# Masking one block of attention rows by multiplication instead of by bias matmuls, in a fused attention and feed-forward kernel

## The chip, the cores and the metric

The kernel runs on one core of a Trainium2 chip. The time is that of one execution on the device, in microseconds (us). TensorE, VectorE, ScalarE, GpSimd and SyncE appear in the profile as PE, DVE, ACT, POOL and SP; PEld is TensorE's weight load.

## The reference

Attention with a band mask of 96 keys, 8 global keys and a slope per head, then a feed-forward layer with a squared ReLU. Cut to what matters:

```python
batch, n_heads, seq, head_dim = (4, 8, 768, 64);  n_global, n_local = (8, 96)
scores = scale * q @ k.T                      # scale = 1/8
dist   = where(is_global & ~is_local, n_local, abs(rel))
scores = where(is_global | is_local, scores - slopes[h] * dist, -1e9)
x = (softmax(scores) @ v)                     # -> (3072, 512)
h = x @ w_in                                  # 512 x 2048
g = s * maximum(h, 0)**2 + b
out = g @ w_out                               # 2048 x 512
```

## The kernel before

The work is cut into 12 **granules** of 256 query rows, three for each of the four batches. They are numbered 0 to 11. The first of each batch (0, 3, 6, 9) has 3 blocks of 128 score columns for each head, the others 4. A **head pair** is two heads; four pairs make a granule. Bias and mask come in one of two ways. Granules 0 and 1 add them in PSUM with a bias matmul ahead of the scores (`SB_mm`); later granules multiply the exponentiated scores by a table `tmpl = exp(slope * base)` on VectorE (`S_mul`), because that table takes time to build and VectorE is free later.

```python
def SB_mm(j, hp, which=None):            # bias by TensorE: 768 or 1024 columns
    ...
    m = base[:].rearrange("p a c -> p (a c)")[:, c0 : c0 + n]
    for hi in range(2):
        nc.tensor.matmul(ps[:, hi, 0:n], lhsT=diag[:, 2 * hp + hi, :], rhs=m, start=True, stop=False)
def S_mul(j, hp):                        # mask by VectorE
    ...
    m = tmpl[:, 2 * hp : 2 * hp + 2, c0 : c0 + n]
    nc.vector.tensor_tensor(pt[:, :, 0:n], pt[:, :, 0:n], m, ALU.mult)
def P1(j, fp, sq="dve", tag="psh"):      # x @ w_in, slice fp of 8, for granule j
    for i in range(2):
        fc = 2 * fp + i
        for kc in range(KC):             # 8 matmuls of 256 columns in all
            nc.tensor.matmul(ps[:, i, :], lhsT=w_in_bf[:, kc, fc * P : (fc + 1) * P], rhs=xT[j][:, kc, :], ...)
    gs = gT[j][:, 2 * fp : 2 * fp + 2, :]
    nc.scalar.activation(gs, ps[:], ACT.Relu)
    ...                                  # and the square, on the engine that sq names
```

The schedule is written by hand: each engine runs its instructions in the order in which the program emits them. The loads of `w_in` come in eight slices, one for each `P1`:

```python
load_v(0); load_quads(1, "k"); load_quads(1, "q")
load_w_in(0, 8); load_w_in(1, 8); load_v(1)
for i in range(2, 8): load_w_in(i, 8)
load_quads(2, "k"); load_quads(2, "q"); load_v(2)
...
idle(9, "av")                            # nine matmuls on constants while the first loads come
...
SB_mm(1, 0);  P1(0, 0, "dve", "pso")     # granule 1's scores among granule 0's products with w_in
SB_mm(1, 1);  S_mm(1, 0, True); S_post(1, 0, True); S_mm(1, 1, True); S_post(1, 1, True)
P1(0, 1)
SB_mm(1, 2);  ...  SB_mm(1, 3);  ...
A(1, 0); A(1, 1, "pso"); P1(0, 2)        # A is P.V: probabilities times v
make_tmpl(0); make_tmpl(1)               # exp of 640 columns for one head, on ScalarE
A(1, 2); P1(0, 3); A(1, 3, "pso"); XT_half(1, 0, "act", "av"); P1(0, 4)
XT_half(1, 1, "dve", "pso"); P1(0, 5)
P1(1, 0); P1(1, 1); P1(1, 2); P1(1, 3)
make_tmpl(2); P1(0, 6)
T_quads(2, "k", ("pso", "av"))           # transposes of granule 2
```

The softmax here doesn't subtract the row's maximum and nothing guards it: scores larger than these inputs give would overflow.

## Time and profile before

| | before |
|---|---|
| time, median of 3 runs | 208.13 us (207.91 to 208.19) |
| span of the traced execution | 205.9 us |
| TensorE, VectorE, ScalarE busy | 97%, 82%, 57% |

The prediction below shows the lines that it rests on. A timeline row gives start, length, engine, line of the program, operation, operands and count; brackets hold the idle time ahead of it and what ended it.

```profile
5.85 0.82 PE L379 MATMUL ps_s<-base,diag 128*128 128x384 bf16 x4
9.29 0.54 PE L446 MATMUL ps_av<-vaug,pt 128*128 128x65 bf16 x12
...
28.13 0.55 PE L288 MATMUL ps_t<-ident,qnat 64*64 64x64 bf16 x32
```

```profile
27.27 0.69 DVE L306 COPY kT<-ps_t 128x512 bf16<-128x512 bf16 x1 [0.20 <-PE ps_t L288]
```

The four bias matmuls of the start take 0.82 us, the first P.V comes at 9.29, and VectorE takes up the transposed keys within 0.5 us of their start at 26.78. The second transposes, at 28.13, wait for nothing.

### The profile page before, as it was taken

Reading aid. Unit: us, or ns where it says so; the run is one execution under the profiler, and the core shown is the slowest. Engines: PE = TensorE matmul, PEld = TensorE weight load, DVE = VectorE, ACT = ScalarE, POOL = GpSimd, SP = SyncE. Lnnn points to the kernel's source line nnn. Section 1 sums busy time; section 2 is a strip of 40 time slices with the busy share of each in tenths; the row PEclk is TensorE's granted clock in tenths of the full one; section 3 lists DMA queues with packets and bytes.
Section 4 is the critical chain, followed back from the end, with each engine's and each line's share of the span. In section 5 each row is a group of like instructions: output and inputs, shape, how many; then the busy total and the mean of one; then the engine's idle time right before and its main releaser. Section 6 shows DMA issues by size and latency. Waiting matters only on the chain.

```text
span 205.9 us, 5605 instructions
## 1 busy us (share of the span) xinstructions
PE 199.9 (97%) x2291; PEld 161.0 (78%) x2299; DVE 169.1 (82%) x409; ACT 118.3 (57%) x181; POOL 73.7 (36%) x98
## 2 busy tenths in 40 slices
PE   7999999999999999999999999999999999999993
PEld 2667886547766678988988988988978988988883
DVE  3685576799989989788799799788799799787693
ACT  5779799455978586536446546546356446424400
POOL 8994673848273019009019029037000000000000
PEclk9999999999999999999999999999999999999999
DMA  5999999999999979999999969979946040050022
GB/s 165 194 183 198 190 194 193 182 148 162 134 125 155 211 112 102 188 159 129 190 128 106 208 82 117 204 114 119 194 80 178 3 135 21 0 153 3 2 105 102
DMA packets 103962, 27.64 MB, mean 134 GB/s; under 512 B 91392, under 2 KB 102016, under 8 KB 103936
## 3 DMA queue, kind: packets, MB, share of 16 engines
q0 software_dynamic: 70976, 13.11, 85.0%
q1 hardware_dynamic: 31904, 13.64, 34.2%
q10 hardware_dynamic: 1056, 0.52, 0.9%
q8 instruction: 18, 0.29, 0.6%
q14 instruction: 8, 0.07, 0.2%
HBM read 27.26 MB, written 6.29 MB: 163 GB/s over the span
## 4 chain that ended last, share of the span: by engine, by line
PE 83%; DVE 8%; ACT 3%; DMA 3%; issue 1%; POOL 0%; SPq 0%; DVEq 0%; ACTq 0%; POOLq 0%
PE ps L528 37%; PE ps_w L702 14%; PE ps_wb L702 6%; PE ps L589 6%; PE ps_av L446 5%; PE ps_s L395 5%; PE ps_wa L702 4%; ACT pt L408 2%; DMA raw<-in_k_dram 2%; PE ps_s L379 2%; DVE xn L464 2%; PE ps_2s L589 2%; DVE pt L418 2%; DMA xT<-xn 1%; DVE o_pr L627 1%
## 5 line engine op out<-in xcount | busy, mean ns | idle before, releaser
L528 PE MATMUL ps<-xT,w_in_bf 128*128 128x256 bf16 x768 | 96.6, 273 | 0.5 <-DVE xn L464 0.2
L528 PEld LDWEIGHTS <-w_in_bf 128*128 128x128 bf16 x768 | 72.7, 98 | 11.4 <-DVE xn L464 0.5
L540 ACT ACTIVATE gT<-ps 128x512 bf16<-128x512 f32 x72 | 43.1, 598 | 58.7 <-PE ps L528 55.9
L408 ACT ACTIVATE pt<-ps_s 128x1024 bf16<-128x1024 f32 (+1 forms) x48 | 43.1, 952 | 2.4 <-PE ps_s L395 2.4
L702 PEld LDWEIGHTS <-sw 128*128 128x128 bf16 x288 | 28.1, 98 | 3.4
L418 DVE TENSOR_TENSOR pt<-pt,tmpl 128x1024 bf16<-128x1024 bf16 (+1 forms) x40 | 25.1, 646 | 2.8 <-ACT pt L408 2.3
L556 DVE TENSOR_TENSOR gT<-gT 128x512 bf16<-128x512 bf16 x68 | 25.8, 415 | 1.8 <-ACT gT L540 1.6
L112 POOL DMA_DIRECT2D vaug<-in_v_dram x24 | 21.5, 913 | 3.9 <-DMA w_out_bf<-in_moe_w_out_dram 1.7
L702 PEld LDWEIGHTS <-gT 128*128 128x128 bf16 x208 | 19.7, 98 | 3.2 <-issue 0.2
L464 DVE TENSOR_TENSOR xn<-ps_av,rc 128x256 bf16<-128x256 f32 x48 | 20.4, 424 | 1.7
L125 POOL COPY pdum<-xT 1x1 bf16<-1x1 bf16 x5 | 3.0, 595 | 49.3 <-DMA xT<-xn 49.3
L589 PE MATMUL ps<-w_out_bf,gT 128*128 128x512 bf16 x74 | 18.8, 379 | 0.4 <-issue 0.2
L702 PE MATMUL ps_w<-tw,sw 128*128 128x256 bf16 x144 | 18.7, 273 | 0.0
L712 DVE SCALAR_TENSOR_TENSOR u<-ps_w,s_bc,bvec 128x256 f32<-128x256 f32 x27 | 12.9, 478 | 6.3 <-PE ps_w L702 6.3
L446 PEld LDWEIGHTS <-pt 128*128 128x128 bf16 x352 | 15.3, 98 | 3.6 <-DVE pt L418 1.2
L538 ACT ACTIVATE gT<-ps 128x512 bf16<-128x512 f32 x24 | 14.2, 599 | 5.1 <-PE ps L528 5.0
L104 POOL DMA_DIRECT2D qnat<-in_q_dram x18 | 16.0, 906 | 2.7 <-PE ps L528 1.8
L104 POOL DMA_DIRECT2D knat<-in_k_dram x18 | 15.9, 893 | 2.1 <-issue 1.6
L446 PE MATMUL ps_av<-vaug,pt 128*128 128x65 bf16 x224 | 16.4, 194 | 0.3 <-DVE pt L418 0.2
L463 DVE RECIPROCAL rc<-ps_av 128x4 f32<-128x4 f32 x48 | 8.7, 181 | 8.8 <-PE ps_av L446 8.5
L589 PEld LDWEIGHTS <-gT 128*128 128x128 bf16 x96 | 8.8, 98 | 8.1
L395 PE MATMUL ps_s<-qT,kT 64*128 64x128 bf16 x224 | 12.5, 218 | 0.0
(99 smaller groups left out, 240.8 us busy)
## 6 DMA issues: line engine op xcount, KB each, us to landing
out_dram<-o_pr SPq DMA_DIRECT2D x10, 512.0 KB, 5.9
vaug<-in_v_dram POOLq DMA_DIRECT2D x24, 128.0 KB, 7.9
knat<-in_k_dram POOLq DMA_DIRECT2D x22, 128.0 KB, 6.1
qnat<-in_q_dram POOLq DMA_DIRECT2D x22, 128.0 KB, 8.0
w_in_bf<-in_moe_w_in_dram POOLq DMA_DIRECT2D x8, 256.0 KB, 7.9
w_out_bf<-in_moe_w_out_dram POOLq DMA_DIRECT2D x4, 512.0 KB, 10.1
out_dram<-o_pr SPq DMA_DIRECT2D x3, 256.0 KB, 2.6
raw<-in_q_dram ACTq DMA_DIRECT2D x2, 256.0 KB, 4.8
```

The source lines that it names most:

```text
L104: nc.gpsimd.dma_start(t[:, i, :, :], src[b, :, sb * P : (sb + 1) * P, :].rearrange("h p d -> p h d"))
L112: nc.gpsimd.dma_start(vaug[b % 2][:, sb, :, 0:D], v[b, :, sb * P : (sb + 1) * P, :].rearrange("h p d -> p h d"),)
L395: nc.tensor.matmul(ps[:, hi, oc * P : (oc + 1) * P], lhsT=kt[r, :], rhs=qT[j][r, hp, i * P : (i + 1) * P], start=not biased, stop=not bias ...
L408: nc.scalar.activation(pt[:, :, 0:n], ps[:, :, 0:n], ACT.Exp, scale=QSCALE)
L418: nc.vector.tensor_tensor(pt[:, :, 0:n], pt[:, :, 0:n], m, ALU.mult)
L446: nc.tensor.matmul(av[:, i, hi, :], lhsT=pt[:, hi, c * P : (c + 1) * P], rhs=vv, start=n_ == 0, stop=n_ == len(ops) - 1,)
L464: nc.vector.tensor_tensor(xn[j][:, :, 2 * hp : 2 * hp + 2, :], av[:, :, :, 0:D], rc[:].to_broadcast((P, GB, 2, D)), ALU.mult,)
L528: nc.tensor.matmul(ps[:, i, :], lhsT=w_in_bf[:, kc, fc * P : (fc + 1) * P], rhs=xT[j][:, kc, :], start=(kc == 0), stop=(kc == KC - 1),)
L540: nc.scalar.activation(gs.rearrange("p f (r t) -> p f r t", r=2), ps[:].rearrange("p f (t r) -> p f r t", r=2), ACT.Relu,)
L556: nc.vector.tensor_tensor(gs, gs, gs, ALU.mult)
L589: nc.tensor.matmul(po[j, tb], lhsT=gT[j][:, fc, tb * P : (tb + 1) * P], rhs=w_out_bf[:, fc, :], start=(fc == 0), stop=(fc == FC - 1),)
L702: nc.tensor.matmul(wt[j, ps], lhsT=lhs[:, f, :], rhs=rhs[:, f, :], start=first and f == 0, stop=f == HF - 1, skip_group_check=True,)
```

## The change

The intent is to take eight bias matmuls off TensorE, the busiest engine, and to mask granule 1 on VectorE. The table must then exist sooner, so it is built by scaling the base for each head on VectorE and two large exps on ScalarE before 6 us; the last part follows in one exp later. Copies that granule 1's scores wait for are made in halves. The order of granule 0's products with `w_in` moves too. The four diagonals that ScalarE made go to VectorE as well, squares of granule 0 are put off (`"late"`, done later by `Q`), and some tiles change their place in PSUM.

```diff
-    base = const.tile([P, 5, P], BF16, name="base")
+    base = const.tile([P, 3, P], BF16, name="base")
...
+    def scale_base(lo, hi):
+        for h in range(H):
+            slope = float(2.0 ** (-8.0 * (h + 1) / H))
+            nc.vector.tensor_scalar_mul(tmpl[:, h, lo:hi, :], base[:, lo:hi, :], slope)
+    def make_tmpl(h0, h1, lo, hi):
+        t = tmpl[:, h0:h1, lo:hi, :]
+        nc.scalar.activation(t, t, ACT.Exp)
+    scale_base(1, 3)
+    make_tmpl(0, 4, 1, 3)
...
     def S_mul(j, hp):
+            m = m[:, :, 1:3, :].rearrange("p h a c -> p h (a c)")
+            x = pt[:].rearrange("p h (i c) -> p h i c", i=GB)
+            nc.vector.tensor_tensor(x, x, m.unsqueeze(2).to_broadcast((P, 2, GB, 2 * P)), ALU.mult)
...
-    SB_mm(1, 0)
-    P1(0, 0, "dve", "pso")
-    SB_mm(1, 1)
-    S_mm(1, 0, True)
-    S_post(1, 0, True)
...
+    S_mm(1, 0)
+    S_post(1, 0, mul=False)
+    P1(0, 0, "late", "pso")
+    VO_prev()
+    S_mm(1, 1)
+    S_post(1, 1, mul=False)
+    VO_own()
+    S_mul(1, 0)
+    P1(0, 1, "late", relu="dve")
+    S_mm(1, 2)
+    S_post(1, 2, mul=False)
+    S_mul(1, 1)
+    P1(0, 2, "late")
+    S_mm(1, 3)
+    S_post(1, 3, mul=False)
+    A(1, 0, norm=False)
+    A(1, 1, "pso", norm=False)
... (P1(0, 3), P1(0, 4), P1(0, 5) each one place earlier as well)
+    P1(0, 6)
     P1(1, 0)
     P1(1, 1)
     P1(1, 2)
     P1(1, 3)
-    make_tmpl(2)
-    P1(0, 6)
+    scale_base(0, 1)
     T_quads(2, "k", ("pso", "av"))
...
-    make_tmpl(5); make_tmpl(6); make_tmpl(7)
+    make_tmpl(0, 8, 0, 1)
```

More of the change, by code (lines that the diff above doesn't have):

```diff
@@ L227 @@
     for h in range(H):
-        make_diag(h, "act" if h >= 4 else "dve")
-    for b in range(2):
-        nc.vector.memset(vaug[b][:, :, :, D : D + 1], 1.0)
-    ones_f = const.tile([P, P], BF16, name="ones_f")
-    nc.vector.memset(ones_f[:], 1.0)
+        make_diag(h, "dve")
     def idle(n, tag="pso", cols=4 * P):
@@ L244, in idle @@
             )
+    nc.vector.memset(base[0:NG, 2, :], -float(NL))
+    tmpl = const.tile([P, H, 3, P], BF16, name="tmpl")
+    def scale_base(lo, hi):
[7 more added lines that the diff above has]
+    make_tmpl(0, 4, 1, 3)
     nc.vector.tensor_copy(base[:, 0, :], base[:, 1, :])
     nc.vector.tensor_scalar_max(base[0:NG, 0, :], base[0:NG, 0, :], -float(NL))
-    nc.vector.memset(base[0:NG, 2, :], -float(NL))
-    nc.vector.tensor_copy(base[:, 3, :], base[:, 2, :])
-    nc.vector.tensor_copy(base[:, 4, :], base[:, 1, :])
-    tmpl = const.tile([P, H, 5 * P], BF16, name="tmpl")
-    def make_tmpl(h):
-        slope = float(2.0 ** (-8.0 * (h + 1) / H))
-        nc.scalar.activation(
-            tmpl[:, h, :], base[:].rearrange("p a c -> p (a c)"), ACT.Exp, scale=slope
-        )
+    for b in range(2):
+        nc.vector.memset(vaug[b][:, :, :, D : D + 1], 1.0)
+    ones_f = const.tile([P, P], BF16, name="ones_f")
+    nc.vector.memset(ones_f[:], 1.0)
     tps = {}
@@ L275, in T_mm, with T_quads @@
                     )
-    def T_quads(j, nm, tags=("psh", "psh"), own=False):
+    def T_quads(j, nm, tags=("psh", "psh"), own=False, both=None):
         a = 0 if nm == "k" else 1
+        if both:
+            t = PS[both].tile([P, 2, 2, 2, GT], BF16, name="ps_t2", tag=both)
+            for half in range(2):
+                tps[j, half] = t[:, half]
         for half in range(2):
@@ L346, in KO, with KO_own, KO_prev, VO_prev @@
         kos[j] = ko
+    def KO_own(half):
+        hs = slice(2 * half, 2 * half + 2)
+        nc.vector.tensor_copy(kos[1][:, hs, 1, NG:P], kT[0][:, hs, 2 * P + NG : 3 * P])
+    def KO_prev():
+        ko = kos[1] = work.tile([P, HP, GB, P], BF16, name="ko", tag="ko", bufs=2)
+        nc.vector.tensor_copy(ko[:, :, 0, NG:P], kT[0][:, :, P + NG : 2 * P])
+        nc.vector.tensor_copy(
+            ko[:, :, :, 0:NG], kT[0][:, :, 0:NG].unsqueeze(2).to_broadcast((P, HP, GB, NG))
+        )
+    def VO_prev():
+        vo = vos[1] = work.tile([P, GB, H, VW], BF16, name="vo", tag="vo", bufs=2)
+        nc.vector.tensor_copy(vo[:, 0, :, 0:65], vaug[0][:, 1, :, 0:65])
+        nc.vector.tensor_copy(vo[0:NG, 0, :, 0:65], vaug[0][0:NG, 0, :, 0:65])
+    def VO_own():
+        vo = vos[1]
+        nc.vector.tensor_copy(vo[:, 1, :, 0:65], vaug[0][:, 2, :, 0:65])
+        nc.vector.tensor_copy(vo[0:NG, 1, :, 0:65], vaug[0][0:NG, 0, :, 0:65])
     def VO(j):
@@ L375, in SB_mm @@
         n = ncols(j)
-        c0 = 0 if n == 3 * P else P
-        m = base[:].rearrange("p a c -> p (a c)")[:, c0 : c0 + n]
+        m = base[:].rearrange("p a c -> p (a c)")
         for hi in range(2):
@@ L390, in S_mm @@
             ko = kos[j]
-            plan = [own[0] + (0,), own[1] + (3,), (ko[:, hp, 0, :], 0, 1), (ko[:, hp, 1, :], 1, 2)]
+            plan = [own[0] + (0,), own[1] + (2,), (ko[:, hp, 0, :], 0, 1), (ko[:, hp, 1, :], 1, 3)]
         for n_, (kt, i, oc) in enumerate(plan):
@@ L414, in S_mul @@
         pt = pts[j, hp]
-        if True:
-            c0 = 0 if n == 3 * P else P
-            m = tmpl[:, 2 * hp : 2 * hp + 2, c0 : c0 + n]
+        m = tmpl[:, 2 * hp : 2 * hp + 2, :, :]
+        if n == 3 * P:
+            m = m.rearrange("p h a c -> p h (a c)")
             nc.vector.tensor_tensor(pt[:, :, 0:n], pt[:, :, 0:n], m, ALU.mult)
+        else:
+            m = m[:, :, 1:3, :].rearrange("p h a c -> p h (a c)")
+            x = pt[:].rearrange("p h (i c) -> p h i c", i=GB)
+            nc.vector.tensor_tensor(x, x, m.unsqueeze(2).to_broadcast((P, 2, GB, 2 * P)), ALU.mult)
     def SS(j, hps, which=None):
@@ L424, in SS, with A @@
             S_post(j, hp)
-    def A(j, hp, tag="av", norm=True):
+    def A(j, hp, tag="av", norm=True, av=None):
         b, g = bg(j)
@@ L431, in A @@
             xn[j] = xpool.tile([P, GB, H, D], BF16, name="xn", tag="xn", bufs=2)
-        av = PS[tag].tile([P, GB, 2, 65], F32, name="ps_av", tag=tag)
+        if av is None:
+            av = PS[tag].tile([P, GB, 2, 65], F32, name="ps_av", tag=tag)
         for i in range(GB):
@@ L441, in A @@
                     ops = [
-                        ((0, 3)[i], vaug[b % 2][:, g * GB + i, h, 0:65]),
-                        ((1, 2)[i], vos[j][:, i, h, 0:65]),
+                        ((0, 2)[i], vaug[b % 2][:, g * GB + i, h, 0:65]),
+                        ((1, 3)[i], vos[j][:, i, h, 0:65]),
                     ]
@@ L519, in flush, with P1 @@
             nc.vector.tensor_tensor(gs, gs, gs, ALU.mult)
-    def P1(j, fp, sq="dve", tag="psh"):
+    def P1(j, fp, sq="dve", tag="psh", relu="act"):
         if j not in gT:
@@ L536, in P1 @@
         flush()
-        if j < W0:
+        if relu == "dve":
+            nc.vector.tensor_scalar_max(gs, ps[:], 0.0)
+        elif j < W0:
             nc.scalar.activation(gs, ps[:], ACT.Relu)
@@ L815 @@
     cast("q", 0)
+    make_tmpl(4, 8, 1, 3)
     T_mm(0, 0, "k")
@@ L841 @@
     S_post(0, 3, True)
+    KO_prev()
     A(0, 0, "pso")
@@ L846 @@
     A(0, 2, "scA")
-    XT_half(0, 0, "act", "pso")
-    A(0, 3, "scB")
-    T_quads(1, "q")
-    T_ev(1, 1, "k", "act")
-    XT_half(0, 1, "dve", "av")
-    KO(1)
-    T_ev(1, 0, "q", "act")
-    T_ev(1, 1, "q")
-    SB_mm(1, 0)
-    P1(0, 0, "dve", "pso")
-    SB_mm(1, 1)
-    S_mm(1, 0, True)
-    S_post(1, 0, True)
-    S_mm(1, 1, True)
-    S_post(1, 1, True)
-    P1(0, 1)
-    SB_mm(1, 2)
-    S_mm(1, 2, True)
-    S_post(1, 2, True)
-    VO(1)
-    SB_mm(1, 3)
-    S_mm(1, 3, True)
-    S_post(1, 3, True)
-    A(1, 0)
-    A(1, 1, "pso")
-    P1(0, 2)
-    make_tmpl(0)
-    make_tmpl(1)
-    A(1, 2)
-    P1(0, 3)
-    A(1, 3, "pso")
+    A(0, 3, "pso")
+    XT_half(0, 0, "act", "av")
+    KO_own(0)
+    T_quads(1, "q", both="scB")
+    T_ev(1, 0, "q", "act")
+    XT_half(0, 1, "dve", "psh")
+    T_ev(1, 1, "k")
+    T_ev(1, 1, "q", "act")
+    KO_own(1)
+    S_mm(1, 0)
[15 more added lines that the diff above has]
+    A(1, 1, "pso", norm=False)
+    S_mul(1, 2)
+    A_norm(1, 0)
+    P1(0, 3, "late")
+    A_norm(1, 1)
+    S_mul(1, 3)
+    A(1, 2, "scA", norm=False)
+    A_norm(1, 2)
+    P1(0, 4, "late")
+    A(1, 3, "scB", norm=False)
+    A_norm(1, 3)
     XT_half(1, 0, "act", "av")
-    P1(0, 4)
+    Q(0, 0)
+    P1(0, 5, "late")
     XT_half(1, 1, "dve", "pso")
-    P1(0, 5)
+    for f in range(1, 6):
+        Q(0, f)
+    P1(0, 6)
     P1(1, 0)
@@ L894 @@
     T_ev(2, 1, "q", "act")
-    make_tmpl(3)
     P1(1, 4)
@@ L898 @@
     VO(2)
-    make_tmpl(4)
     P1(1, 5)
@@ L903 @@
     P1(1, 7)
-    make_tmpl(5)
-    make_tmpl(6)
-    make_tmpl(7)
+    make_tmpl(0, 8, 0, 1)
     po[0, 0] = ps_o.tile([P, DM], F32, name="ps_2", tag="pso")[:]
```

## The prediction

> **What bounds the kernel now.** I read the page's busy shares and its slices first, then the chain that ended last, then the engines' timelines between 9 and 45 us, the stretch that the change touches.
>
> ```profile
> PE 199.9 (97%) x2291; PEld 161.0 (78%) x2299; DVE 169.1 (82%) x409; ACT 118.3 (57%) x181; POOL 73.7 (36%) x98
> PE   7999999999999999999999999999999999999993
> DMA  5999999999999979999999969979946040050022
> PE 83%; DVE 8%; ACT 3%; DMA 3%; issue 1%; POOL 0%; SPq 0%; DVEq 0%; ACTq 0%; POOLq 0%
> ```
>
> TensorE is busy nearly everywhere, and 83% of the chain lies on it: time taken off TensorE shortens the kernel, unless something else then holds TensorE up. The second thing to see is the DMA row: it reads 9 in nearly every slice of the first 75 us, so in the very part where granule 1 is worked the loads run without pause. A TensorE that gets there sooner may find its data not yet landed.
>
> The timeline of TensorE shows the work to be removed (start, length, line, count):
>
> ```profile
> 13.58 0.59 PE L379 MATMUL ps_s<-base,diag 128*128 128x512 bf16 x2
> 15.62 0.59 PE L379 MATMUL ps_s<-base,diag 128*128 128x512 bf16 x2
> 16.54 0.59 PE L379 MATMUL ps_s<-base,diag 128*128 128x512 bf16 x2
> 17.89 1.04 PE L528 MATMUL ps<-xT,w_in_bf 128*128 128x256 bf16 x8
> 19.01 1.03 PE L528 MATMUL ps<-xT,w_in_bf 128*128 128x256 bf16 x8
> 20.35 1.04 PE L528 MATMUL ps<-xT,w_in_bf 128*128 128x256 bf16 x8
> 21.44 5.41 PE L528 MATMUL ps<-xT,w_in_bf 128*128 128x256 bf16 x48
> 26.78 0.45 PE L288 MATMUL ps_t<-ident,knat 64*64 64x64 bf16 x32
> ```
>
> The four L528 rows from 17.89 on are the first products of granule 0 with slices 2, 3, 4 and 5 (with slices 5 and 6 inside the row of 48) of the eight slices of w_in. When did those slices land? The timeline of POOL tells, because eight load semaphores are used in turn: a load waits for the load eight places before it. The loads of granule 2 wait for w_in slices 2 to 5, and those of w_out for slices 6 and 7:
>
> ```profile
> 17.42 0.61 POOL L92 DMA_DIRECT2D qnat<-in_q_dram  x1 [0.60 <-DMA w_in_bf<-in_moe_w_in_dram]
> 18.80 0.61 POOL L92 DMA_DIRECT2D qnat<-in_q_dram  x1 [0.77 <-DMA w_in_bf<-in_moe_w_in_dram]
> 20.10 0.90 POOL L112 DMA_DIRECT2D vaug<-in_v_dram  x1 [0.69 <-DMA w_in_bf<-in_moe_w_in_dram]
> 21.43 0.88 POOL L112 DMA_DIRECT2D vaug<-in_v_dram  x1 [0.44 <-DMA w_in_bf<-in_moe_w_in_dram]
> 23.11 0.75 POOL L135 DMA_DIRECT2D w_out_bf<-in_moe_w_out_dram  x1 [0.80 <-DMA w_in_bf<-in_moe_w_in_dram]
> ```
>
> So slices 2, 3, 4, 5 and 6 have landed by about 17.4, 18.8, 20.1, 21.4 and 23.1 us, one per 1.3 to 1.7 us, and TensorE asks for slices 2 to 5 at 17.9, 19.0, 20.35 and 21.4. The old order is **just in time**: it has 0.5, 0.2, 0.25 and about 0 us to spare. That decides my prediction.
>
> **What the Trainium skill says.** (1) "TensorE: Matmul & The Clock Gate", "Step-by-step: what each phase is for": only weight loads may be pulled ahead, the matmuls stay in program order. The matmuls of the trace follow the emitted order throughout. So one matmul that waits for a slice of w_in holds everything behind it. (2) "Perfetto Trace Analysis", "DMA Instruction — SWDGE (GPSIMD)": the window of such an issue ends when its descriptors are written, not when data has moved. So I take landings from the next issue on the same semaphore; they may be 0.1 to 0.3 us late. The trace agrees that windows are no landings: the page lists w_in issues of some 0.8 us that land 7.9 us after issue. (3) "VectorE: DVE Perf Modes", "What auto-detection actually checks": a bf16 tensor_tensor does two elements a cycle if the innermost step is one. 1024 elements would be 533 ns at 0.96 GHz; the trace has 688 ns alone and 0.60 us from start to start, which agrees. The new mask operand repeats a block of 256 columns with an outer step of zero and an inner step of one, so by that rule it keeps its rate; no run here shows it yet. (4) "TensorE: Matmul & The Clock Gate", "What's actually happening": after an idle window of about 3.4 us the clock is halved. The trace reads 9 for PEclk in all slices, so it shows no such drop yet.
>
> **The change part by part.**
> *Removed from TensorE:* eight 512-column bias matmuls of granule 1. Two take 0.59 us where one takes 0.38, so one costs 0.21 us in a row: 8 x 0.213 = 1.7 us.
> *Added on VectorE:* four multiplications at 0.60, 2.4 us between 14.5 and 20.7 us. VectorE stands idle 2.2 us at 15.65 to 17.85 now, and the squares of granule 0 move behind it. One ReLU moves from ScalarE (0.50) to VectorE (about 0.6). The copies made in halves cost a few fixed parts more, some 0.4 us. None of it is on the path if TensorE waits anyway.
> *ScalarE:* eight exps of 640 columns (0.65 each in a row, 5.2 us) become three of 1024 (0.9 each, 2.7 us): 2.5 us less, mostly in 19.5 to 36 us, where the chain lies on TensorE; worth nothing directly. Two of the exps come before 6 us. VectorE now has 8 scalings of 256 columns there (0.12 each, estimated from 0.09 for 128 columns) and four more diagonals. The cast of k at 4.38 and of q at 4.83, which wait for DMA, may slip by 0.1 to 0.3 us.
> *Moved on TensorE:* the instruction order of the new program with its waits shows the first product with slice 2 already behind the third score product of granule 1, ahead of all four P.V products, where it was behind two of them; and the one with slice 6 ahead of the four products of granule 1, where it was behind them.
>
> Now TensorE in the new order, with durations of the trace: a product (8 matmuls of 256 columns) 0.873, a score product 0.275 plus about 0.1 on the switch, P.V 0.25, transposes 0.22. The last half of xT for granule 0 needs xn of the last head pair (about 11.95), its transposes (12.4) and a VectorE copy (12.8). Score product, product with slice 0 until 13.5, score product until 13.75, product with slice 1 until 14.65, third score product until about 14.9. There, at 14.9, TensorE comes to slice 2, which lands at 17.4: **it stands 2.5 us**. All that was saved before is swallowed, and so is any slip at the start. From 17.45: product 0.87, fourth score product 0.35, two P.V 0.5 (19.2); product with slice 3 (20.05); P.V 0.25; product with slice 4 (21.2); P.V and transposes 0.48; product with slice 5 (22.55); transposes 0.22 (22.75). Slice 6 lands at 22.9 to 23.1: another 0.1 to 0.35 us. Then slice 6 and the four products of granule 1, 5 x 0.873 = 4.37: 27.3 to 27.5. The old kernel is at the same amount of work (eleven products, then the transposes of granule 2) at 26.78. So the new one is there **0.5 to 0.75 us later**, not 1.7 earlier.
>
> After that both do the same TensorE work. From 26.78 to 47 us the chain is almost only TensorE, and the slices of w_out come 0.6 to 0.9 us before they are asked for (32.16, 33.98 and 36.59 against 32.8, 34.8 and 37.5), so a small delay passes through. Between 60 and 76 us the chain goes over VectorE and a DMA, but that stretch starts from TensorE (the bias product at 60.5) and so shifts with it; perhaps 0.1 us is absorbed. Sum: 208.13 + 0.6 - 0.1 = about 208.6 us.
>
> **The rivals.** *(A) The saving comes through.* If the slices could land earlier, TensorE would reach the transposes of granule 2 at about 24.8 us: 1.7 us of bias, 0.3 us of small gaps: 206.1 us. For it: the chain's 83% on TensorE. Against it: the landings follow each other at a steady 187 to 196 GB/s (the windows from 12 to 25 us), and the change leaves the order of loads alone. An early slice 2 alone would not help: slice 6 before the four granule-1 products sets a floor of 27.3 us by itself. *(B) The multiplication with the repeated mask drops to one element a cycle.* Then 0.53 us more in each multiplication of a granule that is not the first of its batch, 8 granules of 4, 32 in all, 17 us; VectorE at 82% would become the bound in parts: 212 to 220 us. Against it: (3) above. I give it 3%. *(C) The stall of 2.5 us halves the clock.* Then 1.7 us or more on top, 210.5 us. It is below the 3.4 us of the skill, and the window has work at both ends: 5%. *(D) The early scalings on VectorE hold up descriptor writing on POOL*, and the slices land later by some tenths: 209 us. POOL has issued its first 15 loads long before they land, so I count on little.
>
> **Range and chances.** The floor by slice 6 is firm within 0.3 us, the carrying to the end within 0.3 us, the runs within 0.15 us. I widen to the fast side for landings read too late and for slack found downstream: 207.5 to 209.4 us. Faster by 2% would need 203.97 us, more than twice all that is removed: 1%. Slower by 2% needs 212.3 us, rival B or a real clock drop: 3%. Within 2%: 96%.
>
> **What would show each step.** Right: no 512-column bias row for granule 1; a TensorE gap of 2 to 3 us before the first product with slice 2, ended at 17.2 to 17.5 us by the w_in load; POOL's issues of granule 2 at the old times within 0.3 us; the transposes of granule 2 at 27.2 to 27.6; multiplications near 690 ns; ScalarE busy about 2.5 us less; PEclk at 9. Wrong: slices landing a microsecond sooner, the transposes of granule 2 before 26.5 us, multiplications near 1.2 us, or a lower PEclk digit in slices 3 to 5.

## The result, and the profile after

| | before | after |
|---|---|---|
| time, median of 4 runs | 208.02 us (207.73 to 208.19) | 208.76 us (208.47 to 208.91) |
| span of the traced execution | 205.9 us | 206.9 us |
| ScalarE busy | 118.3 us | 115.3 us |
| VectorE busy | 169.1 us | 175.9 us |

The ratio of the two is 1.0035, with a 95% interval of 1.0018 to 1.0053. Ratios are computed as the mean time of one kernel's fast runs over that of the other's of the same rounds, so not quite the ratio of the medians quoted. The eight bias matmuls are gone, and the kernel is no faster. The page of the changed kernel: busy time by engine, three rows of the slices, and the chain that ended last by engine.

```profile
PE 199.9 (97%) x2284; PEld 161.1 (78%) x2291; DVE 175.9 (85%) x436; ACT 115.3 (56%) x171; POOL 73.4 (35%) x98
PE   7999989999999999999999999999999999999993
PEclk9999999999999999999999999999999999999999
DMA  5999999999999939999999999999987040050023
PE 80%; DVE 5%; DMA 5%; POOL 5%; ACT 2%; issue 1%; SPq 0%; POOLq 0%; ACTq 0%
```

In the chain, DMA and POOL now hold 10%, where they held 3% and nothing. The chain in order of time tells where (start, length, what; a choice of the pieces):

```profile
8.45 1.65 POOL vaug L112 x2
10.10 7.52 DMA w_in_bf<-in_moe_w_in_dram
17.66 1.05 PE ps L559 x8
27.77 1.08 DVE tmpl L246 x8
```

Up to 17.66 us the kernel now hangs on the load of slice 2 of `w_in`; before, no such load was in the chain. At 27.77 there is a second newcomer: the late scalings of the table. TensorE's timeline shows what they do (compare the rows of the same operations in the prediction and above):

```profile
6.60 1.46 PE L405 MATMUL ps_s<-base,diag 128*128 128x384 bf16 x4
11.31 0.54 PE L477 MATMUL ps_av<-vaug,pt 128*128 128x65 bf16 x12
...
17.66 1.05 PE L559 MATMUL ps<-xT,w_in_bf 128*128 128x256 bf16 x8
19.47 1.04 PE L559 MATMUL ps<-xT,w_in_bf 128*128 128x256 bf16 x8
...
23.02 4.53 PE L559 MATMUL ps<-xT,w_in_bf 128*128 128x256 bf16 x40
27.48 0.45 PE L294 MATMUL ps_t<-ident,knat 64*64 64x64 bf16 x32
27.86 1.05 PE L559 MATMUL ps<-xT,w_in_bf 128*128 128x256 bf16 x8
29.51 0.45 PE L294 MATMUL ps_t<-ident,qnat 64*64 64x64 bf16 x32 [0.60 <-DVE kT L312]
```

Three things are to be seen. The four bias matmuls of the start took 1.46 us instead of 0.82: TensorE ran at half pace there, and the first P.V came 2.0 us late. In spite of that, the transposes of granule 2 are only 0.70 us late (27.48 against 26.78). And a new wait of 0.60 us stands ahead of the second transposes, which makes them 1.38 us late. VectorE's timeline says why: it does the eight scalings before it copies the keys, so the copy comes at 28.77 and not at 27.27.

```profile
27.69 1.16 DVE L246 TENSOR_SCALAR tmpl<-base 128x128 bf16<-128x128 bf16 x8
28.77 0.68 DVE L312 COPY kT<-ps_t 128x512 bf16<-128x512 bf16 x1
```

POOL's timeline, read as in the prediction, gives the landings of slices 2, 4 and 6:

```profile
17.90 0.61 POOL L92 DMA_DIRECT2D qnat<-in_q_dram  x1 [1.72 <-DMA w_in_bf<-in_moe_w_in_dram]
...
20.40 0.89 POOL L112 DMA_DIRECT2D vaug<-in_v_dram  x1 [0.69 <-DMA w_in_bf<-in_moe_w_in_dram]
...
23.07 0.75 POOL L135 DMA_DIRECT2D w_out_bf<-in_moe_w_out_dram  x1 [0.45 <-DMA w_in_bf<-in_moe_w_in_dram]
```

Slices 2 to 5 are 0.3 to 0.5 us later than before (17.42, 18.80, 20.10, 21.43), slice 6 is at the same time (23.11). These times are upper bounds: TensorE starts on slice 2 at 17.66, before the issue at 17.90. Lastly, the group of multiplications of 1024 columns by the table, before and after:

```profile
L418 DVE TENSOR_TENSOR pt<-pt,tmpl 128x1024 bf16<-128x1024 bf16 x28 | 18.6, 685 | 2.4 <-ACT pt L408 2.3
L448 DVE TENSOR_TENSOR pt<-pt,tmpl 128x1024 bf16<-128x1024 bf16 x32 | 21.3, 685 | 1.7 <-ACT pt L434 1.6
```

The mean is 685 ns with the repeated mask and was 685 ns for the 28 of this shape before. So no rate was lost.

Following the lateness through the traced executions: +0.70 us at the first transposes of granule 2, +1.38 at the second, +1.13 from 42 to 79 us (the product row at 42.36 against 41.23, at 79.66 against 78.52), +0.88 at the last matmuls (202.75 against 201.87).

### The profile page after: what moved, and what is told of

The parts are those of the page before. It is cut to its first block, busy times and chain, and to the rows that moved or that the text cites. A ratio compares the mean times of both kernels' runs of the same rounds, so it can differ in the third digit from the quotient of the medians.

```text
span 206.9 us, 5606 instructions
## 1 busy us (share of the span) xinstructions
PE 199.9 (97%) x2284; PEld 161.1 (78%) x2291; DVE 175.9 (85%) x436; ACT 115.3 (56%) x171; POOL 73.4 (35%) x98
## 4 chain that ended last, share of the span: by engine, by line
PE 80%; DVE 5%; DMA 5%; POOL 5%; ACT 2%; issue 1%; SPq 0%; POOLq 0%; ACTq 0%
PE ps L559 37%; PE ps_w L735 15%; PE ps_wb L735 7%; PE ps L622 6%; PE ps_av L477 4%; PE ps_s L421 4%; PE ps_wa L735 4%; DMA w_in_bf<-in_moe_w_in_dram 4%; POOL vaug L112 2%; PE ps_2s L622 2%; DVE pt L448 2%; DMA xT<-xn 1%; DVE o_pr L660 1%; ACT pt L434 1%; POOL w_in_bf L129 1%
## 5 line engine op out<-in xcount | busy, mean ns | idle before, releaser
L573 ACT ACTIVATE gT<-ps 128x512 bf16<-128x512 f32 x72 | 43.1, 598 | 58.5 <-PE ps L559 56.4
L589 DVE TENSOR_TENSOR gT<-gT 128x512 bf16<-128x512 bf16 x74 | 28.0, 415 | 1.7 <-ACT gT L573 1.6
L448 DVE TENSOR_TENSOR pt<-pt,tmpl 128x1024 bf16<-128x1024 bf16 x32 | 21.3, 685 | 1.7 <-ACT pt L434 1.6
L571 ACT ACTIVATE gT<-ps 128x512 bf16<-128x512 f32 x23 | 13.6, 598 | 6.3 <-PE ps L559 6.2
```

The lines of the kernel that those rows point to most:

```text
L448: nc.vector.tensor_tensor(x, x, m.unsqueeze(2).to_broadcast((P, 2, GB, 2 * P)), ALU.mult)
L573: nc.scalar.activation(gs.rearrange("p f (r t) -> p f r t", r=2), ps[:].rearrange("p f (t r) -> p f r t", r=2), ACT.Relu,)
L589: nc.vector.tensor_tensor(gs, gs, gs, ALU.mult)
```

## The experiments

**Theory L** says that the landings of `w_in` and the order of the products set the time: TensorE comes to slice 2 before it has landed, and slice 6 ahead of four other products makes a floor for granule 2; whatever happens earlier is hidden. **Theory S** says that the slower start (more VectorE work before 6 us, TensorE at half pace until 10 us) is what cost the time, since the traced execution shows almost no wait for slice 2. The kernel before ran beside each group, with medians of 207.75, 207.74, 207.97 and 207.90 us.

### e1_start: the start's scalings taken away

```diff
-    scale_base(1, 3)
-    make_tmpl(0, 4, 1, 3)
+    for h in range(3):
+        tmpl_head(h, 1, 3)     # exp of base straight into the table, scale=slope, on ScalarE
...                             # heads 3 to 5 instead of make_tmpl(4, 8, 1, 3); heads 6, 7 ahead of VO_own()
```

> The changed kernel with its start mended: each head's table is one exp straight from the base with the slope as scale, in gaps of ScalarE; the eight scalings of 256 columns on VectorE are gone. Theory L (the landing of the w_in slices sets when TensorE leaves granule 1): the first P.V product comes at about 9.3 us instead of 11.3, TensorE then stands 2 to 2.8 us before the first product with slice 2, which starts at 17.4 to 17.8 as before; the transposes of granule 2 stay at 27.3 to 27.6 us and the time at 208.3 to 208.9. Theory S (the late start, about 2 us, is what the change lost): the transposes of granule 2 come at about 25.5 us and the time is 206.5 to 207.0.

Measured: 209.76 us (208.69 to 209.87, 6 runs), ratio 1.008. The start was repaired, with the first P.V at 9.28 us as in the kernel before, and the kernel got no faster. The runs fall into two groups: four at 209.76 to 209.87 with a mean granted clock of 0.992, and two at 208.69 and 208.81 with 1.0. Even these two are no faster than the changed kernel, where theory S asked for 206.5 to 207.0: theory S falls. Theory L's time (208.3 to 208.9) holds for these two alone. The traced one is of the first group (the page's clock row, then two timeline rows):

```profile
PEclk9996999999999999999999999999999999999999
```

```profile
17.36 1.89 PE L563 MATMUL ps<-xT,w_in_bf 128*128 128x256 bf16 x8 [1.87 <-DMA w_in_bf<-in_moe_w_in_dram]
...
20.60 1.10 PE L563 MATMUL ps<-xT,w_in_bf 128*128 128x256 bf16 x8
```

TensorE stood 1.87 us for slice 2 (2 to 2.8 were expected), and the eight matmuls after that took 1.89 us instead of 1.05. By 20.6 the pace was back. So the half pace held for about 3.2 us, and the transposes of granule 2 came at 28.68, not at 27.3 to 27.6. The Trainium skill ("TensorE: Matmul & The Clock Gate", "What's actually happening") says that the clock doubles after about 3.4 us of sustained work, which agrees with the 3.2 us here (in e9_extra_load below it took about 6); it says that it is halved after an idle window of about 3.4 us, and here the halving followed a wait of 1.87 us. The measurement decides: a wait well under 3.4 us can be enough. One run was traced; that three more ran so is read from their clock and time.

### e11_start_fill: the same with work put into the wait

```diff
+    idle(8, "av")              # on top of e1_start: eight 512-column matmuls on constants
     P1(0, 2, "late")
```

> e1_start with eight idle 512-column matmuls put where TensorE stood 1.87 us waiting for slice 2: 8 x 0.213 = 1.7 us of TensorE work is put back, as much as the eight bias matmuls that the change removed. If the load of slice 2 sets the time there, the added work costs nothing; and if the standing is what halved the pace behind it (four of six runs of e1_start, clock 0.992, 209.8 us), no run shows it any more: 208.6 to 208.9 in all runs, clock 0.997 or more, about 1 us faster than e1_start with more work. If TensorE's own work counted there, the time would rise by up to 1.7 us to 211. If the pace falls for another cause, the runs stay split at 208.7 and 209.8.

```profile
15.86 1.70 PE L232 MATMUL ps_i<-const-bfloat16-1.0 128*128 128x512 bf16 x7 [0.16 <-issue]
17.39 1.04 PE L563 MATMUL ps<-xT,w_in_bf 128*128 128x256 bf16 x8
```

Measured: 208.62 us (208.43 to 208.81, 6 runs, all with a clock of 0.998 or more). One of the eight is missing from the trace. TensorE did 1.7 us more work, just as much as the change had removed, and the median was 1.1 us **lower** than that of e1_start. Against the two runs of e1_start with an undisturbed clock (208.69 and 208.81) nothing changed: work in that place costs nothing, because the next product waits for its load anyway. And with the standing filled no run fell to half pace, against four of six, which points to the standing as its cause. The two ran on different chips; e12_all_again, on the chip of this one, has runs of lower clock too, so the chip alone does not explain it.

### e10_after_again and e2_idle10: does the half pace of the start matter?

e10_after_again is the changed kernel unchanged. e2_idle10 has one more matmul on constants in the gap at the start:

```diff
-    idle(9, "av")
+    idle(10, "av")
```

> The changed kernel itself, unaltered, on the chip of the next three runs, as their yardstick: 1.0035 to 1.005 of the kernel before. Its first trace had TensorE at half pace until about 10 us and no wait of note for slice 2, while e3_row0, whose instructions are the same until 27 us, ran at full pace and waited 1.42 us for it. Theory L: whichever start this trace shows, the transposes of granule 2 come at 27.4 to 27.8 us; a late start has a short wait for slice 2, an early one a long wait.

> The changed kernel with one more idle matmul ahead of the first transposes, so that the TensorE gap before them is about 0.27 us as in the kernel before, instead of 0.69. If the gap is what kept TensorE's matmuls at half pace until 10 us, four 384-column bias matmuls take about 0.8 us as before instead of 1.46 and the first P.V product comes near 9.7 us; if the pace has another cause, it stays near 11.3. Either way theory L expects the time unchanged within 0.3% of the changed kernel (208.3 to 209.0); theory S expects about 207.2 if the pace recovers.

Measured: 208.90 us for e10_after_again (208.73 to 210.58, 4 runs; ratio 1.0072, above the expected 1.0035 to 1.005, mostly because of the one long run), 208.81 for e2_idle10 (208.73 to 208.96, 4 runs; ratio 1.0051). The edit of e2_idle10 did not do what it was made for: its ten matmuls took 3.66 us where the nine had taken 4.00, so the gap before the first transposes grew to 1.03 us and did not shrink to 0.27. Whether the added matmul prevents the half pace can't be told: both kernels left the start at full pace, so with the same instructions the pace varies from execution to execution. Nor is it the length of the gap alone, for 0.69 us stood before the half pace of the first trace and 1.03 us before the full pace here. The 210.58 of one run isn't explained; its mean clock reads 1.0. But the pair of traces of the same kernel is worth more than the question that was asked. TensorE's timeline of e10_after_again:

```profile
6.38 0.82 PE L405 MATMUL ps_s<-base,diag 128*128 128x384 bf16 x4
9.82 0.54 PE L477 MATMUL ps_av<-vaug,pt 128*128 128x65 bf16 x12
...
17.26 1.05 PE L559 MATMUL ps<-xT,w_in_bf 128*128 128x256 bf16 x8 [1.23 <-DMA w_in_bf<-in_moe_w_in_dram]
...
23.18 4.54 PE L559 MATMUL ps<-xT,w_in_bf 128*128 128x256 bf16 x40 [0.39 <-DMA w_in_bf<-in_moe_w_in_dram]
27.65 0.45 PE L294 MATMUL ps_t<-ident,knat 64*64 64x64 bf16 x32
```

The first P.V came 1.5 us sooner than in the first trace of the same kernel (9.82 against 11.31), and the transposes of granule 2 came no sooner (27.65 against 27.48). All of it went into waits for slices 2 and 6. The spans are 207.0 and 206.9 us.

### e4_before_idle6: a late start in the kernel before

```diff
-    idle(9, "av")              # in the kernel before
+    idle(6, "av")
```

> The kernel before with six idle matmuls instead of nine, so that its TensorE too should run at half pace at the start. Both theories expect the first P.V product about 1.5 to 2 us later (10.8 to 11.3 us). Theory L: the kernel before has only 0 to 0.5 us to spare to the slices and no saved work to pay with, so nearly all of it reaches the end: 209.3 to 210 us. If slips at the start are hidden there too, it stays at 208.0 to 208.3.

Measured: 208.74 us (208.60 to 209.13, 4 runs), ratio 1.0049. With three matmuls fewer the start ran at half pace (the four bias matmuls took 1.46 us), and the first P.V came at 10.61, that is 1.32 us late. The lateness was the same at the transposes of granule 2 (28.10, in the row below, against 26.78) and 1.0 us in the time.

```profile
28.10 0.44 PE L288 MATMUL ps_t<-ident,knat 64*64 64x64 bf16 x32
```

The size is below what was expected, because the start slipped less than assumed; the mechanism is as expected. The old order is just in time and passes a slip on; the new order waits for loads and swallows it.

### e3_row0: the late scalings taken off VectorE

```diff
-    scale_base(0, 1)           # eight scalings ahead of the transposes of granule 2
...
-    make_tmpl(0, 8, 0, 1)
...
     XB(4)
+    for h in range(H):
+        tmpl_head(h, 0, 1)     # eight exps on ScalarE, some 10 us later
```

> The changed kernel without the eight late scalings of 128 columns on VectorE (1.08 us at 27.7, right ahead of the eviction of granule 2's kT); that part of the table is made by eight exps with scale on ScalarE at about 40 us, where it stands idle. If these scalings are on the path, the gap of 0.60 us before the second transposes of granule 2 goes and the time falls by 0.4 to 0.6 us to 208.2 to 208.4; if a later wait takes their place, it stays at 208.7.

Measured: 208.03 us (207.71 to 208.42, 6 runs), ratio 1.0011; 0.8 us less than e2_idle10 in the same group, where 0.4 to 0.6 was expected. The two rows of transposes:

```profile
27.71 0.45 PE L298 MATMUL ps_t<-ident,knat 64*64 64x64 bf16 x32
...
29.07 0.45 PE L298 MATMUL ps_t<-ident,qnat 64*64 64x64 bf16 x32
```

The first stand where they stood (27.71 in e2_idle10 as well): the floor of slice 6. The second wait for nothing any more and are 0.66 us sooner than in e2_idle10 (29.73). The gain is there before the exps that moved to about 40 us, so it comes from VectorE and not from them. So eight small instructions on VectorE, which nobody needs for another 10 us, cost the changed kernel 0.8 us by standing in front of one copy.

### e9_extra_load: later slices

```diff
     load_v(1)                  # on top of e3_row0
+    scratch = const.tile([P, KC, DF // 8], BF16, name="scratch")
+    nc.gpsimd.dma_start(scratch[:], w_in_view[:, :, 0 : DF // 8])
     for i in range(2, 8):
```

> e3_row0 with one more load of 256 KB (slice 0 of w_in once more, into a tile that nobody reads) put into the queue ahead of slice 2. No compute instruction changes. Theory L: slices 2 to 6 land 1.3 us later (256 KB at about 195 GB/s), TensorE waits for slice 2 until about 18.7 us and for slice 6 until about 24.4 us, and the time rises by 1.0 to 1.4 us over e3_row0. If TensorE is held by its own work or by VectorE there, the time rises by less than 0.3 us. A longer wait may also halve TensorE's pace for some microseconds, as in e1_start; then more.

Measured: 212.06, 209.35, 211.93 and 210.48 us, with mean clocks of 0.982, 1.0, 0.982 and 0.992. Slice 2 landed about 1.5 us later (the product started at 18.99, after 2.95 us of standing), and the one run with an undisturbed clock is 1.3 us above e3_row0, which is what theory L asks. The other runs lost 1.1 to 2.7 us more, by their clocks to half pace: the traced one is at half pace from 18.99 to about 25 us, without a gap in its work, with clock digits of 7 and 6 in the slices it covers most.

### e5_order: the old order of the products

```diff
     S_mul(1, 1)
-    P1(0, 2, "late")
     S_mm(1, 3)
...                             # P1(0, 2) to P1(0, 5) one place later each, as before
-    P1(0, 6)
     P1(1, 0)
...
     P1(1, 3)
+    P1(0, 6)                   # slice 6 behind granule 1's products again
```

> The changed kernel with the products of w_in put back where they stood in the kernel before: slice 2 behind the fourth score product and two P.V products, slice 6 behind the four granule-1 products; the late scalings stay. Theory L: the wait for slice 2 shrinks from 1.4 to below 0.6 us and the one for slice 6 goes; the transposes of granule 2 come at 26.3 to 27.0 us instead of 27.5 to 27.7, and the time falls by 0.5 to 1.0 us against the changed kernel. If the order is of no account (some other wait holds them), the time is that of the changed kernel.

Measured: 208.41 us (208.00 to 208.47, 5 runs), ratio 1.0024, and 0.5 us less than e10_after_again in the same group. The expectation for the transposes was missed: they came at 27.43, not at 26.3 to 27.0. The waits for `w_in` are gone, as expected, but another took their place. The P.V products waited 0.63 and 0.78 us for VectorE's multiplications, and VectorE's timeline shows what held those up:

```profile
15.74 0.30 DVE L372 COPY vo<-vaug 128x520 bf16<-128x520 bf16 x1 [0.83 <-DMA vaug<-in_v_dram]
```

The copy of v's own rows waits for the load of v, which is queued just before slice 2, and the first multiplication is behind it on VectorE. In the old order, P.V comes sooner than in the new one, and the new chain scores, exp, multiplication, P.V is not ready.

### e6_all and e12_all_again: the three edits together

These are one kernel: e1_start, e3_row0 and e5_order at once.

> All three together: exps straight from the base (as e1_start), no late scalings on VectorE (as e3_row0), the old order of the w_in products (as e5_order). Theory L: TensorE still waits for slice 2, now for under 1 us, and no longer for slice 6; the transposes of granule 2 at about 26.2 us against 26.78 in the kernel before, nothing after them is new, and the time is 0.3 to 0.6 us below the kernel before: 207.1 to 207.5. Were the full 1.7 us of bias to come through, 206.0. If the wait for slice 2 halves TensorE's pace, 208.5 to 209.5.

> e6_all unaltered, to narrow its interval: its first five undisturbed runs had 207.07 to 207.32 and one, with clock 0.989, 209.4. Expected again 207.1 to 207.3 against 207.5 to 208.2 of the kernel before, 0.2 to 0.3% faster, with one run in five or so near 209.4.

Measured for e6_all: 207.24 us (five runs at 207.07 to 207.32, one at 209.40 with a clock of 0.989), ratio 0.999. Its transposes came at 26.64, and the waits for VectorE were 0.65 us in all. Measured for e12_all_again: 208.21 us (206.96 to 209.83), ratio 1.0023; two of its runs, 209.18 and 209.83, have clocks of 0.992 and 0.989. Its trace shows 1.74 us of waiting for multiplications, with the copy of v's rows again waiting (0.86 us) for its load. So the gain of the first measurement is not reliable. The two traces differ in when the load of v lands: in e6_all the copy did not wait for it. That the runs of lower clock are those in which TensorE stood longer is likely, but none of them was traced; the two groups also ran on different chips.

### e13_all_fill: work in those waits

```diff
+    idle(1, "av")              # on top of e6_all
     A(1, 0, norm=False)
+    idle(2, "pso")
     A(1, 1, "pso", norm=False)
```

> e6_all with three idle 512-column matmuls (0.64 us) in its two remaining waits of 0.20 and 0.45 us, which are now for multiplications on VectorE ahead of the first two P.V products. If short standing there is what drops the pace in one run of six, no run is near 209.4 any more and the median stays at 207.1 to 207.4. If the drop comes from elsewhere, runs near 209.4 remain; if the matmuls get into the way, the median rises by 0.1 to 0.3 us.

Measured: 207.68 us (207.34 to 208.08, 6 runs), ratio 0.9993 with 0.9977 to 1.0009; every clock at 0.998 or above. No run in six fell to the lower clock, against three in twelve of e6_all and e12_all_again, which is too few to tell; and no gain is left that is clear of the noise.

### e14_all_vo: the copy of v's rows behind two multiplications

```diff
-    VO_own()                   # on top of e6_all
     S_mul(1, 0)
-    P1(0, 1, "late", relu="dve")
+    P1(0, 1, "late")
...
     S_mul(1, 1)
+    VO_own()
```

> The kernel of e6_all and e12_all_again (each head's table exp on ScalarE, late scalings off VectorE, old order of w_in products), with the copy of v's own rows moved behind the second multiplication of granule 1, and the ReLU of the second product back on ScalarE. Theory: in e12 VectorE's first multiplication stood behind that copy, which waited 0.86 us for a load of v, and TensorE then waited 1 to 2 us in all for the multiplications. With the copy behind them, the waits of the P.V products for VectorE shrink to under 0.6 us in all, the transposes of granule 2 come at 26.0 to 26.7, and the time is 207.0 to 207.4 us, with the runs within 0.4 us of each other. Rival: what TensorE then meets is w_in slices again (the old order is just in time): then a wait of 0.5 to 1.5 us for w_in shows, the transposes come at 26.7 or later and the time is that of the kernel before within 0.2 us.

Measured: 207.63 us (207.25 to 207.67, 5 runs), ratio 0.998 with 0.9967 to 0.9994, clocks at 0.999 or above. Neither expectation holds as written: the transposes came at 27.24, later than the theory asked, and no wait for `w_in` showed, as the rival asked. The wait has moved on once more, to the second part of the same copy:

```profile
17.05 0.19 PE L481 MATMUL ps_av<-vo,pt 128*128 128x65 bf16 x1 [0.64 <-DVE vo L377]
```

With another 0.34 us for a multiplication it makes 0.98 us in all. This is the only version whose interval lies below the kernel before, by 0.2%, with steady runs; it is the best of several tried and was not measured again. It leaves most of the 1.7 us of removed matmuls ungained.

## Why the prediction was right or wrong, point by point

The predicted time was 208.6 us and the measured one 208.76, inside the range and within 2%. The reason given was that the loads of `w_in` and the new order swallow the saving; the experiments bear it out. But two errors of the sum had opposite signs and about the same size, so that the total agrees to 0.2 us is partly luck.

- **The saving of 1.7 us is swallowed by the wait for slice 2:** right, and shown by e11_start_fill (1.7 us of work added in that place cost nothing) and by e10_after_again against the first trace. In the first trace itself the slow start had used up the saving before that wait was reached.
- **"It stands 2.5 us":** the place is right, the size is not. The wait was 1.23 us at a full-pace start (e10_after_again), 1.87 with the start's scalings taken away (e1_start), and 0.3 in the first trace. Two terms of TensorE's path were mis-sized. The first is the start: it was put at 0.1 to 0.3 us of slip, and the first P.V slipped by 0.53 us at full pace (9.82 against 9.29) and by 2.0 in the trace with half pace. The eight scalings of 256 columns took 1.84 us together, not the eight times 0.12 that was estimated, and the casts of k and q came at 4.81 and 5.51 instead of 4.38 and 4.83. The second is the stretch of score products and products with `w_in`. With the start repaired, e1_start still came to slice 2 at 15.49 us (17.36 less the wait of 1.87) and not at 14.9; one score product and one product together took 1.32 us there (12.80 to 14.12), against the 1.15 of the sum (13.5 to 14.65). As the prediction said of all that is saved or lost ahead of slice 2, both were hidden.
- **The floor by slice 6, transposes at 27.2 to 27.6, so 0.5 to 0.75 us late:** right in the first trace (27.48), though no wait stands ahead of the product with slice 6 there, and 0.1 us too early for three others (27.65 to 27.71). e5_order didn't test it alone, because its other wait took over; that slice 6 holds TensorE up is shown by the waits of 0.26 to 0.39 us ahead of that product in e10_after_again, e2_idle10 and e3_row0. With the old order and the two other edits, e6_all has the transposes at 26.64.
- **What was added on VectorE is not on the path:** this step failed. The multiplications, as the prediction had it, cost nothing in the changed kernel, but the late scalings stood in front of the copy of granule 2's keys and made a new wait of 0.60 us on TensorE; e3_row0 shows that they cost 0.8 us. The working had counted VectorE's sum of time and not looked at what each added group stands in front of.
- **"Perhaps 0.1 us is absorbed":** too small. The lateness went from 1.38 us to 0.88 (first trace), from 1.54 to 1.05 (e10_after_again) and from 0.94 to 0.40 (e3_row0). About half of it goes between 29 and 42 us, the rest between 79 us and the end. That second part appears in e4_before_idle6 as well (1.33 to 1.07), so it belongs to the kernel and not to the change; the first part doesn't (1.32 and still 1.33 at 42 us). No wait of over 0.15 us accounts for the first part: in the first trace 0.12 us of it comes back at the second transposes, which are followed sooner by the next product (0.37 us against 0.49), and the rest in the rows from 34 to 37 us. Where the second part comes back wasn't looked for. Of the three landings of `w_out` that the prediction read, one is none: POOL's issue at 32.16 had waited for TensorE and not for a load. No wait of TensorE for `w_out` shows in the traces after the change, so nothing hung on it. Together with the step above this is why the total came out: 0.6 us too little added, 0.4 too little taken off.
- **Rival A, the saving comes through:** out, as argued. e5_order shows why the old order would not bring it either: behind the loads stands the chain through VectorE and the load of v. What the prediction named for this rival, slices that land earlier, no run tried; e9_extra_load tests only later ones.
- **Rival B, half rate of the multiplication:** out, 685 ns before and after.
- **Rival C, the stall halves the clock:** given 5%, since 2.5 us is below 3.4. In the changed kernel itself it didn't show in the four runs of the result (208.47 to 208.91 us), where the late start kept the wait short (0.3 us in the trace); a run of e10_after_again with 210.58 us stays unexplained, and its clock of 1.0 does not rule out half pace, as the last point says. One edit away, with a wait of 1.87 us, four runs of six had it, at a cost of 1.05 us. The reasoning with a fixed threshold was wrong.
- **Rival D, POOL's issues are held up:** the issues behind slices 2 to 5 came 0.3 to 0.5 us later in the first trace, a little beyond the 0.3 that was named; slice 6, which makes the floor, was not later. In e10_after_again it is the other way round: the issues behind slices 2 to 5 are within 0.08 us of the old times and the one behind slice 6 is 0.3 us later (23.41). No run isolates the cause.
- **ScalarE about 2.5 us less, the clock digits at 9:** 3.0 us less, and 9 throughout, though the row reads 9 also where the start ran at half pace.

## What to carry to other kernels

Before taking work off the busiest engine, look up when the data of its next instructions land: where loads come just in time, removed work turns into waiting, and a test with added filler work shows it at once. For work that moves to another engine, ask which instruction it stands in front of, rather than how busy that engine is; and watch waits of about two microseconds on TensorE: here one of 1.87 us was followed by half pace, which cost another microsecond.

## What the Trainium skill lacked or had wrong

- "TensorE: Matmul & The Clock Gate" puts the halving of the clock after an idle window of about 3.4 us. Here a wait of 1.87 us was followed by half pace (eight matmuls in 1.89 us instead of 1.05; four of six runs of e1_start), while waits of 1.23 to 1.42 us were not followed by it in the three traces that have them. For waits shorter than that window the page gives no length. The return to full pace, which it puts after about 3.4 us of sustained work, took 3.2 us in e1_start and about 6 us in e9_extra_load.
- The same page says that the slow start varies from run to run, and the traces agree (four bias matmuls in 1.46 or 0.82 us with the same instructions). It also warns that the clock events of a profile are not to be trusted fully, but not that they can miss a slow start whole: the row read 9 in every slice of the execution with 1.46 us.
